# A quarter of one weight piece moved from a casting software load to an uncast hardware load and a POOL cast

## The chip, the cores and the metric

One core of a Trainium2 chip runs the kernel. The metric is the device time in microseconds (us). The span in a profile is about 1.8 us shorter than the time of the same run.

Three words are used throughout. A *software load* is a DMA that POOL issues; here it also casts float32 to bfloat16 on the way. A *hardware load* is a DMA that SP issues; it doesn't cast. A *landing* is the moment at which one of the 16 DMA engines adds its part to a transfer's semaphore. Every transfer waited for here needs all of its engines, so its *last* landing is what a consumer sees.

## The reference

Two stages follow each other: a windowed attention (half of the heads with a plain window of 32, half with a dilated one), and a soft mixture of experts on its result.

```python
# q, k, v: (8, 8, 576, 64) float32; phi: (512, 32); w1: (8, 512, 1024); w2: (8, 1024, 512)
attn = softmax(mask(q @ k.T / 8)) @ v               # per batch and head
x = attn.transpose(0, 2, 1, 3).reshape(4608, 512)
logits = x @ phi
slot_input = softmax(logits, axis=0).T @ x          # 8 experts, 4 slots each
for e in range(8):
    slot_out[e] = relu(slot_input[e] @ w1[e]) @ w2[e]
out = softmax(logits, axis=1) @ slot_out            # (4608, 512) float32
```

All inputs are float32 and are read once: 28.3 MB of q, k, v and 33.6 MB of weights.

## The kernel before

The program is written as a list of operations with modelled durations, which a small list scheduler in the kernel file orders for each engine. Inputs come in 16 halves (batch and head group). The software queue carries them and, in between, pieces of w1 and then of w2:

```python
def w1_piece(e, hf, r0=0, n=2):
    def fn():
        return pool.dma_start(                      # float32 in DRAM to bfloat16 in SBUF
            a(o_w1 + e * 4096 + hf * 2048 + 1024 * r0, [[1, 1024 * n]]),
            moe_w1[e, 256 * hf:256 * hf + 256, :].rearrange("(p two) f -> p (two f)", two=2)
            [:, 1024 * r0:1024 * (r0 + n)])
    return (fn, n << 19, f"w1_{e}{hf}", [b_w1[e]])
...
for e in range(8):
    wq += [w1_piece(e, x) for x in range(e == 0, 2)]     # w1_01 is the first of them
for e in range(6):
    wq += [w2_piece(e, 0), w2_piece(e, 4)]
for s in range(2):                                       # the last weights: slabs of 256 columns
    wq += [w2_slab(6, s), w2_slab(7, s, 0, 4), w2_slab(7, s, 4, 2),
           w2_slab(7, s, 6, 1), w2_slab(7, s, 7, 1)]
```

The very first w1 piece already goes another way: SP loads it uncast at the start, and ACT casts it. A small hardware load brings phi; it is issued after the first transpose on DVE.

```python
op(SP, lambda: spq.dma_start(
    af(w2off(4), [[1, 2048]]),
    moe_w1[0, 0:256, :].rearrange("(p two) f -> p (two f)", two=2)), .1, -200.0,
   kind="dma", nbytes=1 << 20, sem=sem("s_w1f"), writes=b_w2[4], name="w1f")
...
def load_phi(first):
    op(SP, lambda: spq.dma_start(
        f(o_phst, [[64, 2], [1, 64]]),
        moe_phi.rearrange("(hf p two) s -> p hf (two s)", hf=2, two=2)), .1, 20.0,
       kind="dma", nbytes=65536, sem=sem("s_phi"), writes=[b_phst], name="phi", after=[first])
```

After the last slab of w2 come the last matmul of the experts (L858), an addition on DVE (L882), and 46 output matmuls (L902) with their evictions on ACT (L911) and DVE (L914) and the stores.

The softmax here doesn't subtract the row's maximum and nothing guards it: scores larger than these inputs give would overflow.

## Time and profile before

| | before |
|---|---|
| time, median of the first 3 runs | 178.28 us |
| span of the profile | 176.3 us |
| busy: PE, DVE, ACT, POOL | 72%, 68%, 59%, 29% |
| software queue, share of 16 engines' span | 91.4% |

The first lines are from the page of the kernel before: the DMA engines' busy tenths and GB/s in 40 slices of the span, and the DMA queues with packets, MB, and the time that the packets took as a share of 16 engines' span.

```profile
DMA  5999999999999999999999999999999999999997
GB/s 182 237 211 213 216 207 213 214 209 213 215 208 214 214 208 214 214 207 215 210 209 213 211 211 216 213 216 210 217 213 211 210 192 194 298 319 415 416 427 316
...
q0 software_dynamic: 15056, 30.41, 91.4%
q1 hardware_dynamic: 4144, 10.55, 15.6%
q8 instruction: 16, 0.26, 0.5%
```

The DMA engines are busy 90% or more from the second slice to the last but one. While the casting loads run they write some 212 GB/s, and as a cast halves the bytes they read twice that. No compute engine is near its limit. So the DMA engines bound the kernel, and the end of the chain of waits (start, duration, what) shows where this ends:

```profile
119.16 33.35 DMA ar<-in_moe_w_dram
152.51 0.04 issue
152.56 0.30 PE ps L858
152.85 0.02 issue
152.88 0.44 DVE ar L882
...
153.81 8.63 DVE ar L914 x15
```

The last slab lands at 152.51 us, and everything after it follows at once. From there to the end of the span it takes 23.8 us. The landing of the last slab sets the time.

The profile has no view for the next step; it comes from the semaphore updates in the trace. For the last slab, the 16 engines' landings, in us after the first of them:

```
before: 0.00 0.02 0.15 0.16 0.21 0.45 0.50 1.09 2.07 2.26 2.31 2.33 2.34 2.35 2.41 2.47
```

For the early loads the same list spans 0.3 us. It grows in steps. The 16 packets of q8 above are instruction fetches of 16 KB; each took 0.89 to 0.97 us, and four fetches of 8 KB on another queue took 0.32 us each. Sixteen steps of 1 us fit eight engines that fetched twice, which are then over 2 us late. The trace supports this: the first late landing, 1.2 us behind, comes at the load that lands just after the first fetch (23.9 us), the fetch at 80.8 us takes one engine from 1.28 to 2.42 us, and the eight durations of the fetches repeat in the same order within 1 ns. The four fetches of 8 KB fit the three engines in between (0.45, 0.50 and, after two of them, 1.09 us). As each engine always has more loads queued, it never catches up, and everyone waits for the late eight.

### The profile page before, as it was taken

The page shows a single profiled execution, that of the slowest core. Times are in us where ns is not written, and L with a number is a line of the kernel's source. Part 1 is how long each engine was busy: PE and PEld are TensorE (multiplying, and loading weights), DVE is VectorE, ACT ScalarE, POOL GpSimd, SP SyncE. Part 2 cuts the span into 40 slices and gives each one's busy share as a digit, 9 for nine tenths or more (in the row PEclk, how much of TensorE's full clock was granted, in tenths as well). Part 3 has the DMA queues.
Part 4 walks back from the last instruction along what each step waited for, and adds up shares of the span by engine and source line. Part 5 has one row for each costly group of instructions (what it writes and reads, how often), then busy time and mean ns, then how long its engine had stood idle before and what let it go on. Part 6 is the DMA issues. An engine that isn't in the chain of part 4 may idle for free.

```text
span 176.3 us, 4802 instructions
## 1 busy us (share of the span) xinstructions
PE 126.7 (72%) x2102; PEld 85.4 (48%) x2102; DVE 119.6 (68%) x218; ACT 104.3 (59%) x165; POOL 51.1 (29%) x102
## 2 busy tenths in 40 slices
PE   0008787889798999989969989996685648897000
PEld 0005555667577767667647667674333224431000
DVE  6899396897989899999599899655400013499200
ACT  2404379888689889799669779793320012399000
POOL 7659822422422513423860000691000000000000
PEclk9999999999999999999999999999999996999855
DMA  5999999999999999999999999999999999999997
GB/s 182 237 211 213 216 207 213 214 209 213 215 208 214 214 208 214 214 207 215 210 209 213 211 211 216 213 216 210 217 213 211 210 192 194 298 319 415 416 427 316
DMA packets 19221, 41.26 MB, mean 234 GB/s; under 512 B 1921, under 2 KB 8577, under 8 KB 18305
## 3 DMA queue, kind: packets, MB, share of 16 engines
q0 software_dynamic: 15056, 30.41, 91.4%
q1 hardware_dynamic: 4144, 10.55, 15.6%
q8 instruction: 16, 0.26, 0.5%
q14 instruction: 5, 0.03, 0.0%
HBM read 61.93 MB, written 9.44 MB: 405 GB/s over the span
## 4 chain that ended last, share of the span: by engine, by line
DMA 47%; DVE 21%; PE 13%; POOL 4%; ACT 4%; issue 2%; POOLq 0%; DVEq 0%
DMA ar<-in_k_dram 28%; DMA ar<-in_moe_w_dram 19%; DVE ar L489 6%; DVE ar L914 6%; PE ps L510 4%; POOL ar L371 3%; ACT ar L549 3%; PE ps L604 2%; DVE ar L615 2%; PE ps L571 2%; DVE ar L445 2%; PE ps L517 2%; DVE ar L450 1%; PE ps L527 1%; DVE ar L495 1%
## 5 line engine op out<-in xcount | busy, mean ns | idle before, releaser
L549 ACT ACTIVATE ar<-ps 128x1152 bf16<-128x1152 f32 (+1 forms) x32 | 37.9, 1185 | 24.1 <-PE ps L534 13.4
L489 DVE STREAM_TRANSPOSE ar<-ar 128x576 uint32<-128x576 uint32 x40 | 48.6, 1241 | 3.0 <-DMA ar<-in_k_dram 2.8
L510 PE MATMUL ps<-ar 128*128 128x320 bf16 (+1 forms) x128 | 23.4, 308 | 15.7 <-DVE ar L489 13.8
L615 DVE TENSOR_TENSOR ar<-ps,fs 96x768 bf16<-96x768 f32 (+1 forms) x32 | 26.3, 822 | 1.2
L577 ACT ACTIVATE ar<-ps 128x768 bf16<-128x768 bf16 x32 | 24.9, 812 | 1.1 <-PE ps L571 1.0
L510 PEld LDWEIGHTS ps<-ar 128*128 128x128 bf16 x128 | 10.4, 100 | 20.8 <-POOL ar L418 13.7
L604 PE MATMUL ps<-ar 128*128 128x65 bf16 x320 | 15.5, 197 | 3.4 <-ACT ar L549 3.2
L571 PE MATMUL ps<-ar 128*128 128x128 bf16 x192 | 15.8, 228 | 2.8 <-DVE ar L615 1.9
L911 ACT ACTIVATE ar<-ps,fs 128x512 f32<-128x512 f32 (+1 forms) x23 | 11.5, 637 | 8.2 <-PE ps L902 8.2
L604 PEld LDWEIGHTS ps<-ar 128*128 128x128 bf16 x320 | 12.8, 100 | 6.5 <-ACT ar L549 3.8
L858 PE MATMUL ps<-ar 128*32 128x512 bf16 (+1 forms) x80 | 11.4, 352 | 5.9 <-DMA ar<-in_moe_w_dram 5.2
L335 POOL DMA_DIRECT2D ar<-in_k_dram x16 | 8.9, 554 | 23.1 <-DVE ar L489 19.7
L571 PEld LDWEIGHTS ps<-ar 128*128 128x128 bf16 x192 | 12.4, 118 | 4.3 <-DVE ar L615 2.5
L914 DVE TENSOR_SCALAR ar<-ps,fs 128x512 f32<-128x512 f32 (+1 forms) x23 | 12.7, 626 | 1.2 <-PE ps L902 1.2
L611 DVE RECIPROCAL fs<-ps 96x12 f32<-96x12 f32 (+1 forms) x32 | 6.4, 199 | 9.9 <-PE ps L604 9.3
L364 POOL DMA_DIRECT2D ar<-in_moe_w_dram x12 | 6.4, 580 | 20.8 <-DVE ar L489 20.8
L335 POOL DMA_DIRECT2D ar<-in_q_dram x16 | 8.7, 546 | 11.9 <-DVE fs L611 7.0
L902 PE MATMUL ps<-ar 128*128 128x512 bf16 (+1 forms) x46 | 10.4, 356 | 1.3 <-DVE ar L882 1.0
L335 POOL DMA_DIRECT2D ar<-in_v_dram x16 | 8.8, 549 | 8.9 <-DVE fs L611 5.5
L858 PEld LDWEIGHTS ps<-ar 128*32 128x32 bf16 x80 | 5.1, 99 | 12.0 <-DMA ar<-in_moe_w_dram 9.0
L671 ACT ACTIVATE ar<-ps 128x576 bf16<-128x576 bf16 x16 | 9.9, 656 | 1.4 <-PE ps L655 1.2
L694 PE MATMUL ps<-ar 128*128 128x288 bf16 x64 | 9.2, 287 | 1.2 <-ACT ar L678 1.2
(75 smaller groups left out, 190.6 us busy)
## 6 DMA issues: line engine op xcount, KB each, us to landing
ar<-in_moe_w_dram POOLq DMA_DIRECT2D x29, 512.0 KB, 27.0
out_dram<-ar SPq DMA_DIRECT2D x6, 1024.0 KB, 8.5
ar<-in_k_dram POOLq DMA_DIRECT2D x16, 288.0 KB, 21.1
ar<-in_q_dram POOLq DMA_DIRECT2D x16, 288.0 KB, 21.3
ar<-in_v_dram POOLq DMA_DIRECT2D x16, 288.0 KB, 21.6
out_dram<-ar SPq DMA_DIRECT2D x10, 256.0 KB, 3.5
ar<-in_moe_w_dram SPq DMA_DIRECT2D x1, 1024.0 KB, 4.8
ar<-in_moe_w_dram POOLq DMA_DIRECT2D x2, 256.0 KB, 33.0
```

What stands on the lines that cost most here:

```text
L335: return pool.dma_start(a(o_stg + (s * 3 + j) * 1152, [[1, 1152]]), src[b, 4 * dl:4 * dl + 4].rearrange("h (p t) d -> (h p) (t d)", p=32))
L489: return dve.transpose(au(o_dst, [[1, 18], [18, 32]]), au(src, [[32, 18], [1, 32]]))
L510: pe.matmul(pf(h, 0, [[1, W]]), a(o_id, [[1, 128]]), a(msk, [[1, W]]), start=True, stop=False)
L549: eo = op(ACT, lambda P=P, W=W: act.activation(a(P, [[W, 4], [1, W]]), AP(ps, 0, [[4096, 128], [512, 4], [1, W]]), ACTF.Exp, scale=SCALE), ...
L571: last = pe.transpose(pb(bank.idx, bb * 256 + par * 32, [[64, 4], [1, 32]]), src, a(o_id, [[1, 128]]))
L577: op(ACT, lambda t=t, bank=bank: act.activation(a(o_vb[vs] + 3 * t * VBK, [[66, 12], [2, 32], [1, 2]]), pb(bank.idx, 0, [[64, 12], [1, 32] ...
L604: last = pe.matmul(pf(bank.idx + x, 65 * t, [[1, 65]]), w, a(VB + t * VBK + 66 * h, [[1, 65]]), start=True, stop=True)
L615: op(DVE, lambda hp=hp, bank=bank: dve.tensor_tensor(a(ox + 128 * hp, [[64, 2], [256, NT], [1, 64]], 0, rows), pf(bank.idx, 0, [[512, 2], ...
L858: last = pe.matmul(pf(sobank[x].idx, 0, [[1, n]], 32 * j, 32), a(o_htz + 1024 * g + 128 * c + 32 * j, [[1, 32]]), a(w2off(e) + DM * c + co ...
L902: op(PE, lambda: pe.matmul(pf(bank.idx, 0, [[1, cw]]), a(o_et + 512 * G + j, [[4, 128]]), a(o_so + c0, [[1, cw]]), start=True, stop=True), ...
L911: op(ACT, lambda: act.activation(dst, src(), ACTF.Copy, scale=sca), actt(cw, .1), prio + .1, reads=[bank, b_rinv], writes=wr, name=f"OE{G} ...
L914: op(DVE, lambda: dve.tensor_scalar(dst, src(), sca, None, op0=AluOp.mult), dvet(cw, True) + .08, prio + .1, reads=[bank, b_rinv], writes= ...
```

## The change

Of the piece w1_01 (128 partitions, 8 KB of float32 each), 96 partitions stay in the software queue. The other 32 are loaded uncast by one hardware transfer into space where w2 comes later, and POOL casts them. The source is written with an outer size of 4. We read this as meant to let only four DMA engines carry it: those that the fetches leave free, if it is chosen well.

```diff
-    def w1_piece(e, hf, r0=0, n=2):
+    def w1_piece(e, hf):
+        pn = 96 if (e, hf) == (0, 1) else 128
+
         def fn():
             return pool.dma_start(
-                a(o_w1 + e * 4096 + hf * 2048 + 1024 * r0, [[1, 1024 * n]]),
-                moe_w1[e, 256 * hf:256 * hf + 256, :].rearrange("(p two) f -> p (two f)", two=2)
-                [:, 1024 * r0:1024 * (r0 + n)])
-        return (fn, n << 19, f"w1_{e}{hf}", [b_w1[e]])
+                a(o_w1 + e * 4096 + hf * 2048, [[1, 2048]], 0, pn),
+                moe_w1[e, 256 * hf:256 * hf + 256, :].rearrange("(p two) f -> p (two f)", two=2)[:pn])
+        return (fn, pn << 13, f"w1_{e}{hf}", [b_w1[e]])
...
+    def load_w1g(after):
+        src = moe_w1[0, 448:512, :].rearrange("(n p two) f -> n p (two f)", n=4, two=2)
+        op(SP, lambda: spq.dma_start(af(w2off(3), [[1, 2048]], 96, 32), src), .1, -50.0, kind="dma",
+           nbytes=1 << 18, lag=4.0, sem=sem("s_w1g"), after=[after], writes=b_w2[3], name="w1g")
+        op(POOL, lambda: pool.tensor_copy(
+            a(o_w1 + 2048, [[1, 2048]], 96, 32), af(w2off(3), [[1, 2048]], 96, 32)), 2.5, 0.0,
+           reads=b_w2[3], writes=[b_w1[0]], name="w1gc")
...
+        if i == 1:
+            load_w1g(first_t[3])
```

## The prediction

> **What bounds it.** The DMA engines. In the page's slices they are busy 90% or more from 4.4 us to the end. The software queue takes 91.4% of 16 engines' span. The chain of waits holds a 33.35 us DMA piece on the w tensors ending at 152.51, when the last w2 slab lands; then come the last L858, L882, L902, 8.6 us of L914 and the stores. PE (72%), DVE (68%), ACT (59%) and POOL (29%) have gaps. So a change of w1 loading counts only by how it moves the landing of the last w2 slab.
>
> **The engines do not finish together.** Each load's semaphore gets 16 engine updates. In the trace they lie within 0.3 us for early loads, but spread to 1.4 us at 36 us, 2.4 us at 96 us, and 2.46 us for the last slab: seven engines at 0 to 0.5 us, one at 1.05, eight at 2.05 to 2.46. The DMA table has 16 instruction packets of 16 KB, 0.89 to 0.97 us each, and four of 8 KB (0.32 us) after the start; the spread grows in such steps. I read this as eight engines that fetched instructions twice each and, with a queue that never empties, never catch up.
>
> **The change.** 32 of 128 rows of w1_01 leave the software queue: each of 16 engines loses two 8 KB rows, about 0.30 us each (a 4 KB cast packet), so 0.6 us. The same 256 KB come by a hardware transfer from SP. The Trainium skill, "DMA: Bandwidth & Descriptors", section "Why a DMA increments its semaphore by 16 and not by 1", says the engine count is the largest up to 16 that divides both outer sizes, and hardware transfers use the lowest-numbered engines: here 32 and 4, so engines 0 to 3, eight 8 KB packets each. Such packets took 0.31 us in w1f: 2.5 us. Net (estimate): four engines +1.9 us, twelve -0.6 us.
>
> If engines 0 to 3 are early ones (this profile names no engines; the outer size of 4 looks chosen for it), the late ones end at 2.46 - 0.6 = 1.86 and the four at 0.15 + 1.9 = 2.05: the last slab lands 0.2 to 0.5 us sooner, all on the chain. If they are late ones, up to 1.9 us later.
>
> **Off the chain.** POOL gains a 32x2048 cast, by L418 (three 128x512 in 1.63 us) an estimated 2.2 us; POOL idles 3 to 4 us between loads, and 20 us of transfers are queued, so later issues cost nothing. The transfer is issued near 16 us and should land near 22 us (phi took 6.4 us there). The loads of half 2 land up to 2 us later, near 18 to 20 us; DVE takes them up at 23.05, so no stall. The scheduler's new times may reorder instructions: some tenths, either sign.
>
> **Prediction.** 177.9 us (178.28 less 0.4), 8 in 10 between 177.3 and 178.9. Faster by over 2%: 0.01; within 2%: 0.96; slower: 0.03.
>
> **What would show it.** Right: the spread at the last slab falls from 2.46 to about 2 us, the last wait for w ends 0.2 to 0.5 us before 152.5, the output phase keeps its length. Wrong: a spread of 4 us (late engines hit: near 180 us); a new gap of DVE or PE at 17 to 30 us; POOL held by the cast so long that DMA share drops.
>
> **What would make it wrong.** Engines 0 to 3 late; the transfer spread on 16 engines (no gain at all); reordering that costs more than the balance gains.

## More of the kernel before

The Trainium skill, "Runtime: NRT & Kernel Launch", section "Instruction fetch mechanics", says that instructions are fetched in blocks of 16 KiB by a DMA queue of the sequencer's own, and that what a block boundary costs is "mostly hidden". The size agrees with this trace. What the fetch takes of a DMA engine isn't hidden here: that engine has no time to spare.

Last, the hardware loads of SP in the first 40 us (timeline: start, duration of the issue):

```profile
0.74 0.38 SPq L399 DMA_DIRECT2D ar<-in_moe_w_dram  x1
11.85 0.39 SPq L466 DMA_DIRECT2D fs<-in_moe_phi_dram  x1
```

## The result, and the profile after

| | before | after |
|---|---|---|
| median | 178.23 us (178.01 to 178.52, 6 runs) | 178.44 us (178.27 to 179.39, 6 runs) |
| ratio, 95% interval | | 1.0023 (0.9999 to 1.0048) |
| span of the profiled run | 176.3 us | 177.6 us (a run of 179.39 us) |
| last slab: first and last landing | 150.05, 152.51 us | 150.23, 153.72 us |

A ratio is the mean time of one kernel's fast runs over that of the other's of the same rounds, so not quite the ratio of the medians quoted. The profile after fell on the slowest of its six runs; a second one, of a run of 178.76 us, is read below.

The queues, and the issues of weight loads (count, KB each, us from issue to landing), after:

```profile
q0 software_dynamic: 15024, 30.28, 90.6%
q1 hardware_dynamic: 4192, 10.81, 15.9%
q8 instruction: 16, 0.26, 0.5%
...
ar<-in_moe_w_dram POOLq DMA_DIRECT2D x1, 384.0 KB, 11.4
ar<-in_moe_w_dram SPq DMA_DIRECT2D x1, 256.0 KB, 6.1
```

The software queue has 32 packets less, one for each row. The hardware queue has 48 more: 32 packets of 8 KB and 16 of 4 bytes, which in this trace are the completion writes. Sixteen completion writes are those of 16 engines. On four there would be four, and 36 packets more.

The end of the chain of waits after:

```profile
119.92 33.09 DMA ar<-in_moe_w_dram
153.02 0.04 issue
153.06 0.39 PE ps L871 x2
153.46 0.02 issue
153.48 0.28 PE ps L871
153.76 0.01 issue
153.77 0.30 PE ps L871
154.06 0.02 issue
154.09 0.44 DVE ar L895
...
155.02 8.64 DVE ar L927 x15
```

The chain's DMA piece ends here with a slab before the last, at 153.02 us; the last slab lands at 153.72 us, just before the matmul at 153.77. The same instructions follow it (L871, L895 and L927 are L858, L882 and L914 of before), and from 153.72 us to the end of the span there are again 23.9 us. The time was lost before the last slab landed, not in the output.

The transfer on SP, and the cast on POOL (timeline):

```profile
11.85 0.38 SPq L477 DMA_DIRECT2D fs<-in_moe_phi_dram  x1
15.81 0.34 SPq L413 DMA_DIRECT2D ar<-in_moe_w_dram  x1
```

```profile
33.12 1.89 POOL L415 CAST ar<-ar 32x2048 bf16<-32x2048 f32 x1
```

The cast took 1.89 us (2.2 were estimated). It can't be the cause of the loss: the landings of the loads are shifted from 21 us on, before the cast runs at 33 us, and from 24 to 107 us the mean shift stays at 0.4 to 0.7 us. Nor can the order of instructions: in the two built programs the order on PE, DVE and ACT is the same, instruction for instruction. POOL has one cast more, at another place between its loads, and SP one transfer more.

### The profile page after: what moved, and what is told of

The parts are those of the page before. It is cut to its first block, busy times and chain, and to the rows that moved or that the text cites. A ratio compares the mean times of both kernels' runs of the same rounds, so it can differ in the third digit from the quotient of the medians.

```text
span 177.6 us, 4804 instructions
## 1 busy us (share of the span) xinstructions
PE 127.5 (72%) x2102; PEld 85.8 (48%) x2102; DVE 119.4 (67%) x218; ACT 104.5 (59%) x165; POOL 53.0 (30%) x103
## 3 DMA queue, kind: packets, MB, share of 16 engines
q1 hardware_dynamic: 4192, 10.81, 15.9%
## 4 chain that ended last, share of the span: by engine, by line
DMA 47%; DVE 20%; PE 15%; ACT 5%; POOL 3%; issue 2%; POOLq 0%; DVEq 0%
DMA ar<-in_k_dram 28%; DMA ar<-in_moe_w_dram 19%; DVE ar L927 6%; DVE ar L500 5%; PE ps L521 4%; ACT ar L560 3%; POOL ar L372 2%; DVE ar L626 2%; PE ps L615 2%; DVE ar L456 2%; PE ps L528 2%; PE ps L582 1%; PE ps L705 1%; PE ps L666 1%; PE ps L538 1%
## 5 line engine op out<-in xcount | busy, mean ns | idle before, releaser
L521 PE MATMUL ps<-ar 128*128 128x320 bf16 (+1 forms) x128 | 22.8, 302 | 16.5 <-DVE ar L500 13.8
L615 PE MATMUL ps<-ar 128*128 128x65 bf16 x320 | 15.1, 195 | 3.4 <-ACT ar L560 3.2
L335 POOL DMA_DIRECT2D ar<-in_k_dram x16 | 8.9, 554 | 23.8 <-DVE ar L500 14.3
L871 PE MATMUL ps<-ar 128*32 128x512 bf16 (+1 forms) x80 | 12.3, 376 | 4.3 <-DMA ar<-in_moe_w_dram 3.6
L927 DVE TENSOR_SCALAR ar<-ps,fs 128x512 f32<-128x512 f32 (+1 forms) x23 | 12.7, 628 | 1.2 <-PE ps L915 1.2
L871 PEld LDWEIGHTS ps<-ar 128*32 128x32 bf16 x80 | 5.4, 104 | 11.1 <-DMA ar<-in_moe_w_dram 7.7
## 6 DMA issues: line engine op xcount, KB each, us to landing
ar<-in_k_dram POOLq DMA_DIRECT2D x16, 288.0 KB, 23.8
```

What stands on the lines that cost most here:

```text
L335: return pool.dma_start(a(o_stg + (s * 3 + j) * 1152, [[1, 1152]]), src[b, 4 * dl:4 * dl + 4].rearrange("h (p t) d -> (h p) (t d)", p=32))
L521: pe.matmul(pf(h, 0, [[1, W]]), a(o_id, [[1, 128]]), a(msk, [[1, W]]), start=True, stop=False)
L615: last = pe.matmul(pf(bank.idx + x, 65 * t, [[1, 65]]), w, a(VB + t * VBK + 66 * h, [[1, 65]]), start=True, stop=True)
L871: last = pe.matmul(pf(sobank[x].idx, 0, [[1, n]], 32 * j, 32), a(o_htz + 1024 * g + 128 * c + 32 * j, [[1, 32]]), a(w2off(e) + DM * c + co ...
L927: op(DVE, lambda: dve.tensor_scalar(dst, src(), sca, None, op0=AluOp.mult), dvet(cw, True) + .08, prio + .1, reads=[bank, b_rinv], writes= ...
```

## The experiments

In the built program, the source of the hardware transfer is no longer what was written. The lines are the patterns (step, count) of its two sides, as the instruction carries them:

```
written:  moe_w1[0, 448:512, :] as (n p two) f -> n p (two f), n=4     sizes 4 x 8 x 2048
built:    DRAM [[2048, 32], [1, 2048]]     SBUF [[52370, 32], [1, 2048]]
```

The four groups of eight rows are contiguous in DRAM, so the step of 4 and the step of 8 became one step of 32 when the instruction was built. The Trainium skill, "DMA: Bandwidth & Descriptors", section "Why a DMA increments its semaphore by 16 and not by 1", says that the engine count comes from the slowest dimensions of both sides "as the instruction carries it"; the largest count up to 16 that divides 32 and 32 is 16. The 16 completion writes agree.

From this comes theory A: every engine gives up two rows in the software queue and gets two back by hardware, so nothing is balanced. Its rival B: the transfer does run on four engines, and the gain is given back elsewhere. A second question soon joined it: why the change isn't the same as before but slightly *slower*.

In the table, the shift is that of the last slab's landing (first engine, mean of 16, last engine) against the mean of the two profiles of before, 150.02, 151.38 and 152.54 us. Ratios are against the kernel before on the same chip, five rounds (for r1 to r12). The batches r1 to r4, r5 to r8 and r9 to r12 ran on three different chips, so a shift may hold a difference of chips, and a ratio doesn't. By the margin of 2% every verdict is "same"; what follows is about tenths of a per cent.

| run | ratio (95%) | range of times, us | shift: first, mean, last, us |
|---|---|---|---|
| r1 before again | 0.9998 (0.9986 to 1.0010) | 178.13 to 178.65 | |
| the change, first profile | 1.0023 (0.9999 to 1.0048) | 178.27 to 179.39 | +0.21 +0.54 +1.19 |
| r2 change again | 1.0038 (1.0018 to 1.0058) | 178.26 to 179.64 | +0.09 +0.33 +0.49 |
| r3 eight transfers of 4 neighbours | 1.0125 (1.0096 to 1.0154) | 179.41 to 181.37 | -0.55 +0.35 +1.65 |
| r4 four transfers of 8 neighbours | 1.0157 (1.0144 to 1.0170) | 181.02 to 181.39 | +1.08 +2.05 +2.96 |
| r5 eight transfers of 4, 8 apart | 1.0020 (1.0008 to 1.0032) | 178.58 to 178.77 | -0.69 +0.03 +0.52 |
| r6 four transfers of 4, 4 apart | 1.0005 (0.9993 to 1.0017) | 178.29 to 178.55 | -0.22 +0.14 +0.22 |
| r7 no transfer | 0.9980 (0.9962 to 0.9997) | 177.59 to 178.50 | -0.48 -0.13 +0.21 |
| r8 transfer 30 us later | 1.0050 (1.0019 to 1.0081) | 178.44 to 180.43 | +0.04 +0.05 +0.29 |
| r9 change, phi early | 1.0002 (0.9987 to 1.0017) | 178.14 to 178.83 | -0.03 -0.02 -0.05 |
| r10 before, phi early | 0.9980 (0.9968 to 0.9992) | 177.99 to 178.12 | -0.15 -0.11 -0.09 |
| r11 r6, phi early | 0.9977 (0.9964 to 0.9989) | 177.80 to 178.30 | -0.30 -0.05 -0.41 |
| r12 r7, phi early | 0.9962 (0.9949 to 0.9975) | 177.48 to 177.98 | -0.74 -0.73 -0.71 |

In all fourteen profiles the span ends 23.8 to 24.0 us after the last landing, so the last column is the change of the profiled run's time. The shift belongs to one run each, the ratio to all of them.

### r1 and r2: both kernels again

No edit.

> Control, the kernel before unchanged, run as if it were a change. Both theories: ratio 1.000 within 0.002; it tells how far two sets of runs of one program differ, and whether the 2.46 us spread of the 16 engines' landings at the last w2 slab (seven early, one between, eight late) comes again in another profile.

> The change unchanged, for a tighter ratio. Theory A (the transfer runs on all 16 engines, two 8 KB packets each, so every engine reads as many bytes as before): ratio 1.000 within 0.002, spread at the last slab as in before, 2.4 to 2.5 us; the first profile's 3.5 us was a one-time stall of four packets of up to 1.5 us at 14 to 16 us and does not come again. Rival B (it runs on 4 engines and the gain is given back elsewhere, by the POOL cast or by sharing): 32 packets of 8 KB take at least 2.5 us from the first start to the last end, and the spread is 2.0 us or the late group is another.

The kernel before repeats: its second profile has the last slab's landings at 0.00 to 0.57 for seven engines, 1.17 for one, 2.29 to 2.56 for eight. The change is 0.4% slower, outside the 0.002 that theory A allowed; both theories missed this. Its times are also wider than those of before. Rival B's mark, at least 2.5 us for the 32 packets, isn't met: in the two profiles of the change they run from 19.3 to 21.1 and from 19.4 to 21.5 us. "Won't come again" was wrong too: of the software packets between 15 and 19 us, which take 0.19 us each, four took 0.8 to 1.5 us in the first profile, and three took over 0.5 us in the second.

### r3 and r4: engine counts of 4 and 8 by small transfers

```diff
-        src = moe_w1[0, 448:512, :].rearrange("(n p two) f -> n p (two f)", n=4, two=2)
-        op(SP, lambda: spq.dma_start(af(w2off(3), [[1, 2048]], 96, 32), src), ...)
+        sg = sem("s_w1g")
+        for x in range(8):                                  # r4: range(4), 8 partitions each
+            p0 = 96 + 4 * x
+            src = moe_w1[0, 256 + 2 * p0:256 + 2 * p0 + 8, :].rearrange("(p two) f -> p (two f)", two=2)
+            op(SP, lambda p0=p0, src=src: spq.dma_start(af(w2off(3), [[1, 2048]], p0, 4), src), ...)
```

> The same 32 rows on 8 transfers of 4 partitions each, so that the engine count can only be 4. Theory A: the packets now take 2.5 us or more instead of 1.7, four engines gain 1.9 us and twelve lose 0.6 us. If engines 0 to 3 are early ones: last slab sooner by 0.2 to 0.5 us, ratio 0.997 to 0.999 against before. If they are late ones: later by about 1.9 us, ratio 1.010. Rival B: the same as the change in spread and time.

> The same 32 rows on 4 transfers of 8 partitions each: engine count 8, four packets each. Net: eight engines +0.6 us, eight -0.6 us. If engines 0 to 7 are the early ones: last slab sooner by 0.6 us, ratio 0.9965, spread 1.3 us or less. If they are the late ones: later by 0.6 us, ratio 1.0035, spread 3.7 us. If they are mixed: no gain. Rival B: no difference from the change beyond 0.1 us.

The hardware queue in r3, and its issues on SP:

```profile
q1 hardware_dynamic: 4208, 10.81, 16.1%
...
15.80 2.66 SPq L416 DMA_DIRECT2D ar<-in_moe_w_dram  x8
```

There are 64 packets more than in before: 32 of data and 8 times 4 completion writes. So these transfers do run on four engines each, and rival B falls. In the landings of r3, twelve engines stand together once the transfer is through and four stand apart; at the last slab:

```
30.6 us on: 0.00 0.01 0.04 0.07 0.08 0.12 0.13 0.19 0.23 0.23 1.25 1.86 | 3.45 4.40 4.45 4.46
last slab:  0.00 0.15 0.21 0.23 2.17 2.20 2.24 2.30 2.31 2.32 2.33 2.35 | 3.70 4.42 4.65 4.72
```

Eight of the twelve become the late engines (2.17 to 2.35). So the four with the transfer are *early* engines, as the prediction hoped. But four early ones of the twelve are left at 0.23 us or less, so the four include those that stood at 0.45, 0.50 and 1.09 us before. And they paid too much: eight packets should have cost 2.5 us, yet the last engine came 1.65 us later than before. In r3 the median 8 KB packet took 0.46 us, not 0.31, and some took 0.9. In r4 the mean was 0.76 us, software packets took up to 0.79 us at the same time, and at the last slab even the first of the 16 landings came 1.08 us later. None of the three cases expected for r4 came.

### r5 and r6: four engines, but not on neighbouring partitions

The Trainium skill, "SBUF — State Buffer", section "Door 1: The DMA port swizzle", says that four neighbouring partitions share one of 16 DMA ports. In r3 the four engines of one transfer write four neighbours. So theory C: they held each other up. Its rival D: a hardware packet costs that much on a busy engine anyway.

```diff
+        for x in range(8):                                  # r6: range(4), rows of partitions 0 to 15, 4 apart
+            src = moe_w1[0, 448:512, :].rearrange("(n p two) f -> n p (two f)", n=4, two=2)[:, x, :]
+            dst = AP(ar_f.tensor, ((96 + x) * NBF + w2off(3)) // 2, [[8 * (NBF // 2), 4], [1, 2048]])
+            op(SP, lambda dst=dst, src=src: spq.dma_start(dst, src), ...)
```

> Engine count 4 again, but each of the 8 transfers takes every eighth partition (96+x, 104+x, 112+x, 120+x), as a single transfer with an outer size of 4 that had not been merged would do: no two of the four engines write neighbouring partitions. Theory C (in r3_four the four engines held each other up because they wrote 4 neighbouring partitions at a time; alone a packet costs 0.31 us): 8 KB packets of 0.31 to 0.35 us, four engines +1.9 us and twelve -0.57 us against before, last slab 0.5 us later than before, ratio 1.003. Rival D (a hardware packet on a busy engine costs 0.47 us wherever it writes): as r3_four, four engines +3.2 us, ratio 1.012.

> Half the size: rows of partitions 0 to 15 by four transfers of 4 partitions 4 apart, 112 rows by software (7 per engine). Theory C: four engines +0.94 us, twelve -0.3 us; the four are early ones (0 to 1.1 us in before), so the last slab lands 0.3 us sooner, ratio 0.998. Rival D: four engines 4 x 0.47 - 0.3 = +1.6 us, the worst of them at 1.1 + 1.6 against 2.47: last slab 0.2 us later, ratio 1.001.

Theory D falls, and C holds as far as this goes. With the same bytes on four engines, the quartiles and the maximum of the packets' times in r5 are all 0.32 us, and the ratio goes from 1.0125 to 1.0020. But r5 changed more than the partitions: the four rows of one transfer are 64 KB apart in DRAM, not 8 KB, and SP issued the transfers 0.6 us apart, not 0.3. That the ports are the cause is not shown apart from these two. Near 28 us the first landing came 0.64 us sooner than before. Ten of the twelve other engines stood 0.5 to 0.9 us ahead of the mean of before's 16 there, and the four stood 1.8 to 1.9 us behind it. The end of the chain in r5:

```profile
119.23 33.83 DMA ar<-in_moe_w_dram
153.06 0.04 issue
153.10 0.30 PE ps L874
```

So this is the change as it was meant, with a measured gain on twelve engines, and the last slab still lands 0.52 us *later* than before (153.06 us). The four engines fell back by 1.9 us on top of up to 1.1 us that they already had. (Followed from load to load, the 3.44 below is a late engine that a held-up packet of 0.96 us near 15.5 us put back; the last, 3.73, is one of the four.)

```
r5: 0.00 0.07 0.29 0.44 2.22 2.27 2.29 2.36 2.37 2.41 2.43 2.77 3.10 3.12 3.44 3.73
```

Half the size (r6) should then have gained 0.3 us, and didn't: 1.0005, with the last slab 0.22 us later. These are the numbers that D gave, but not by D's cause: the packets took 0.32 us, not 0.47. Its profile has held-up software packets again, four of 0.47 to 0.96 us near 15.8 us, and its late engines spread from 2.2 to 2.96.

### r7 and r8: the software side alone, and another time

r7 leaves the hardware transfer out (POOL fills the rows with others, so its result is wrong on purpose). r8 issues it after the k transpose of half 5. In both, the durations in the scheduler's model were kept at those of before, so that PE, DVE and ACT keep their order.

```diff
-        op(SP, lambda: spq.dma_start(af(w2off(3), [[1, 2048]], 96, 32), src), ...)      # r7
-            a(o_w1 + 2048, [[1, 2048]], 96, 32), af(w2off(3), [[1, 2048]], 96, 32)), ...)
+            a(o_w1 + 2048, [[1, 2048]], 96, 32), a(o_w1, [[1, 2048]], 96, 32)), ...)
```

```diff
-        if i == 1:                                                                      # r8
-            load_w1g(first_t[3])
+        if i == 5:
+            load_w1g(first_t[15])
```

> The 96-row software load alone: no hardware transfer at all, POOL copies rows of the first w1 piece in place of the missing 32 (wrong result on purpose). Theory A: all 16 engines 0.57 us earlier, same spread of 2.5 us, ratio 0.9967. It measures what the software side gives back; what the hardware transfer adds is the change less this. If the 96-row load itself unbalanced the engines, the spread would be 3 us and the ratio 1.000.

> The change, but the hardware transfer is issued 30 us later (after the k transpose of half 5), away from phi and the start. Theory E (the change's extra 0.6 us over nothing is the crowding of phi, the shortened load and this transfer at 15 to 21 us): ratio 1.000 to 1.001. Rival F (the transfer itself costs more on the 16 engines, 0.8 to 1.0 us, than the 0.57 us that it saves): ratio 1.003 as in r2_after_again.

r7's times fall into two groups, three runs at 177.6 to 177.7 and three at 178.1 to 178.5. Its profile is of the second (178.45 us) and has six software packets of 0.8 to 1.3 us at 15.5 to 15.7 us. So the hold-ups don't need the new transfer. They come where the shortened w1_01 ends and phi starts.

The profile of r8 happens to have none, and shows both halves of the sum. Until 46 us the loads land 0.62 us sooner on the mean of 16 engines; when the transfer has passed, 0.07 us later. So the software side gives 0.62 us and the transfer takes 0.69 us. Yet r8's times reach 180.43 us, and its ratio of 1.0050 misses E's 1.000 to 1.001 (F's 1.003 lies in its interval, though F had the transfer at 0.8 us or more). Neither explains the slowest runs, and no profile fell on one. As phi is at its old place in r8, these runs may have hold-ups by phi too.

### r9 to r12: phi at the start

In before, the packets of phi (256 bytes each) start at 15.4 us though phi is issued at 11.85, just when the last packets of w1_01 start (15.8). In the change both come 0.3 to 0.6 us sooner. Theory G: small packets of phi at the end of the shortened load hold up single packets of the next one. The test moves phi away; it is then issued at 1.2 us and its packets are all done by 5.5 us. The only reordering is that DVE casts phi earlier.

```diff
-            load_phi(first_t[0])
+            load_phi(None)
```

> The change with the phi load issued at the start, behind the first w1 piece, in place of 11.85 us. Theory G (the wide and longer times of the change, 178.3 to 179.6, come from single software packets of up to 1.5 us held up at 15 to 18 us, where the small packets of phi meet the end of the shortened w1 load): no software packet over 0.45 us before 19 us, runs within 0.3 us of each other, ratio 1.000 to 1.001 (the transfer adds 0.69 us to every engine and the software load gives back 0.57 to 0.63). Rival H (the shortened load or the hardware transfer do it without phi): still 178.3 to 179.6, ratio 1.003.

> The kernel before with phi issued at the start: the control for r9. Theory G: in the kernel before phi costs little where it is, so ratio 1.000 within 0.0015.

> 16 rows on four engines, 4 partitions apart, and phi at the start. Theory C with G: twelve engines -0.3 us, four early ones +0.95 us, no held-up packets: last slab 0.3 us sooner, ratio 0.998, spread 2.5 us with the four between 1 and 2.2 us. Rival H: as r6, ratio 1.0005.

> 96 rows by software, no hardware transfer (wrong result on purpose), phi at the start. Theory G: all 16 engines 0.57 to 0.63 us sooner, every run within 0.3 us, ratio 0.9967. Rival H: two groups of times, 177.6 and 178.5, as r7.

In none of the four profiles does a software packet of the inputs between 11 and 19 us take over 0.3 us. The change becomes the same as before (1.0002), r7 gains its full 0.7 us (0.9962, shifts of -0.74, -0.73 and -0.71, of which 0.1 us is what phi gives before too), and r6 gains. With phi at its old place and the load shortened, six of eight profiles have an input packet of over 0.5 us between 15 and 17 us; r3 and r8 have none, so r3's loss isn't this. The ends of the chain in r9, r11 and r12 are the last weights:

```profile
118.60 33.19 DMA ar<-in_moe_w_dram
```

```profile
118.81 33.32 DMA ar<-in_moe_w_dram
152.13 0.04 issue
```

```profile
118.45 33.38 DMA ar<-in_moe_w_dram
151.83 0.04 issue
```

The last slab lands at 152.13 us in r11 and at 151.83 in r12; in r9 the chain's last weights piece is one slab earlier, and the last slab lands at 152.49. r9 against r12 is the hardware transfer alone: 0.71 us on the mean of 16 engines, with nothing else disturbed.

The landings of the change add up the same way. When the shortened load lands, the mean of 16 engines is 0.67 us ahead of before in its first profile and 0.62 us in its second. By the last load before the transfer, 0.26 and 0.38 us of that are left; the time that input packets took over their usual 0.19 us accounts for 0.39 of the 0.41 us lost in the first profile, and for 0.13 of the 0.24 us in the second. After the transfer the mean is 0.55 and 0.34 us behind.

Three expectations of G were missed. r9 still has two runs of six at 178.75 and 178.83 us, so the range is 0.69 us and not 0.3; r12's is 0.50. And r10 isn't within 0.0015 of before but 0.2% faster: phi costs something in the kernel before too. One of the two profiles of before (r1) does have one packet of the inputs of 0.75 us, near 15.9 us.

This bears on what r9 shows. Early phi gains about 0.2% in the kernel before as well, so like with like, both with phi early, the change is still about 0.2% slower: 1.0002 against 0.9980, medians of 178.27 and 178.09 us (the two intervals overlap a little). The profiles have 0.09 us of this on the mean of 16 engines (shifts of -0.02 and -0.11), near the 0.07 us by which the transfer costs more than it saves in r8; much of the rest is in r9's two slow runs, which aren't explained.

r11 is faster than both kernels (0.9977). But r10, which moves phi and nothing else, has 0.9980. In r11's profile the last slab lands 0.32 us sooner than in r10's (152.45), as C with G says; over all runs the two can't be told apart, as two of r11's five took 178.2 and 178.3 us. What is shown to beat before is the earlier phi, by 0.2%.

## Why the prediction was right or wrong

The time was predicted as 177.9 us, between 177.3 and 178.9, and the same within 2%. It was 178.44 us, and the same. The number held, but its reason didn't: the gain of 0.4 us that was expected isn't there, and the median rose by 0.21 us. That the time lies in the range is luck: the range was wide enough to hold a change that gains nothing.

- *"What bounds it. The DMA engines."* Right. In all fourteen profiles, the time after the last landing is 23.8 to 24.0 us, and the time of a run follows its last slab.
- *"The engines do not finish together."* Right, and repeated: seven early, one between, eight late at the last slab in both profiles of before.
- *"here 32 and 4, so engines 0 to 3."* This is the step that failed. The outer size of 4 is in the source only; the built instruction carries 32 and 32, and 16 engines took two packets each. So no engine was relieved: each saved about 0.62 us of software load and paid about 0.69 us for the transfer (r8). The prediction named this under what would make it wrong ("the transfer spread on 16 engines (no gain at all)"), but gave it no weight in the 0.4 us. No run was needed to see it: the pattern of the built instruction shows it. (The trace doesn't name the engines, so "0 to 3" itself isn't checked.)
- *"Net (estimate): four engines +1.9 us, twelve -0.6 us."* Right for a transfer that does run on four engines and doesn't write neighbours: +1.9 and -0.64 us in r5.
- *"If engines 0 to 3 are early ones ... the four at 0.15 + 1.9 = 2.05."* Mis-sized. They are early ones (r3), but not all at 0.15: they include the ones at 0.45, 0.50 and 1.09 us. In r5 the last landing came 0.52 us later. So even with four engines the change would have lost, as r5 did (1.0020).
- *"POOL ... later issues cost nothing"* and *"no stall"*. Right. The cast took 1.89 us, the shift of the landings was there before it, and in the profile of the change the time after the last landing is unchanged.
- *"reordering that costs more than the balance gains."* There was none on PE, DVE and ACT.
- Not foreseen: hold-ups of single packets where phi meets the shortened load. One engine that is held up for a microsecond stays behind to the end. In the change's two profiles 0.41 and 0.24 us of the lead go in that stretch. Over all runs their share of the 0.2 to 0.4% isn't settled: r9 takes it away, but early phi helps the kernel before by 0.2% too (r10).

Left open: what makes some runs with a hardware transfer of 32 neighbouring partitions slow (r8 up to 180.43 us, with phi late; r9 up to 178.83), as no profile fell on such a run; what exactly holds up a packet when phi passes; whether ports, DRAM rows or the pace of issue made r3's packets slow; and what explains r4, where even the first landing came 1.08 us later.

## What to carry to other kernels

When all 16 DMA engines are busy to the end, ask which engine is last, not how many bytes there are: moving bytes pays only if the last engine loses some, and what holds the last one up is paid in full. If a transfer is meant for fewer engines, look at the pattern of the built instruction, or count its completion writes, before believing the source; and try rows and partitions that are not neighbours for engines that work together (here 1.0020 against 1.0125). Try small hardware loads before the software queue is full (here 0.2% for phi).

## What the Trainium skill lacked or had wrong

- "DMA: Bandwidth & Descriptors": its rule of the engine count held in every run (16, 4 and 8 completion writes per transfer for outer sizes of 32, 4 and 8). It lacks the warning that an outer size which is contiguous with the next one can be gone from the built instruction: 4 x 8 became 32.
- "SBUF — State Buffer": the runs fit its port map, though they don't test it alone. The page has a rate for one transfer of 1 MiB on one port, but nothing for small packets of several engines on one port. Four engines on four neighbouring partitions took 0.46 us for the median 8 KB packet, and 0.32 us when the partitions were 8 apart; the kernel's ratio was 1.0125 and 1.0020.
- "Runtime: NRT & Kernel Launch": the cost of a block boundary is called "mostly hidden", and what a fetch takes of a DMA engine isn't counted. Here each fetch of 16 KB takes a DMA engine for 0.89 to 0.97 us, and with full queues two of them leave eight engines over 2 us late at the end.
- No page has the hold-up of software packets by a small hardware load: up to 1.5 us for a packet of 0.19 us, as phi passed at the end of a load; it was gone with phi at the start.
- "DMA: Bandwidth & Descriptors" says in "Queues, rings and completion order" that an engine changes between queues only at packet boundaries. The runs can't test this, as the trace names no engines, but they have a number that the page lacks: a hardware load issued into full queues started late. Phi was issued at 11.85 us and its first packet started at 15.1 to 15.6 us, and the transfer of w1 waited 3.4 to 4.0 us; the first load, into empty queues, waited 1.0 us.
